# Seven products for eight in the first product of a second feed-forward layer, with streamed operands

## The chip, the core and the metric

The program runs on one core of a Trainium2 chip. The metric is the device time of one execution, in microseconds (us), as a median over runs. The core has five engines that run side by side and wait for each other by semaphores: TensorE (PE, with PEld for the loading of its stationary operand), VectorE (DVE), ScalarE (ACT), GpSimd (POOL) and SyncE (SP), which issues the transfers here. The matrix products go to eight banks of PSUM (128 partitions x 512 float32 each); all else lies in SBUF or in DRAM.

## The reference

An attention is followed by two feed-forward layers on 2304 tokens; the change is in the second layer alone. Its first product sums over 512 inputs, its second over 2048.

```python
'moe2': n_tokens, d_model, d_ff = (2304, 512, 2048)

def _moe2_ref(x, w_in, w_out):
    h = x @ w_in
    sp = np.where(h > 20.0, h, np.log1p(np.exp(np.minimum(h, 20.0))))
    g = h * np.tanh(sp)
    return (g @ w_out).astype(np.float32)
```

The first layer has the same sizes with `g = h / (1 + exp(-1.702 h))`. The weights are float64 in DRAM; the kernel sees them as pairs of 32-bit words.

## The kernel before

**Precision.** Each operand of a product is split into a high part (rounded to the matmul's float32r form) and a low part (the rest). A product of two operands is three matmuls: high by high, high by low, low by high. A "unit" is what one f (one of 16 blocks of 128 of the 2048 hidden columns) does for one block of tokens.

**Layers 1 and 2.** Both walk over five blocks of tokens, 512, 512, 512, 512 and 256, and in each over the 16 f. The first product of f (`mm_h`, L538) is 12 matmuls: four chunks of the 512 inputs (K) by three, into one of four PSUM banks h0 to h3. The second product is 12 matmuls too (L583 in layer 1, L957 in layer 2) into four accumulators tb0 to tb3, which add up over the 16 f. In layer 1 a unit h1(f) is followed, two units later, by o1(f); between them ScalarE and VectorE make `g` and split it (L564 to L570). In layer 2 the f go in pairs (G = 2): VectorE copies h out of its bank (L901) and cuts it at 20 (L904), ScalarE takes exp, log and, one pair later, tanh (L919, with a load of a function table at two of the three), VectorE multiplies and splits (L929 to L936), and the second product of a pair comes DEPTH = 3 pairs behind its first. At a block's end the accumulators are copied (L969) and stored (L972).

**Weights.** The 16 pairs of tiles wh(f), wl(f), called W0 to W15 below, lie in SBUF: each holds 512 columns for the first product and 512 for the second. The weights of layer 1 are converted from the float64 words (`conv_w`): SP loads them into a raw buffer `sr`; ScalarE writes a value and a remainder (L397, L399); VectorE clips and shifts (L403, L406), GpSimd adds (L409), VectorE sets the sign (L411); all on 128x1024, in a value buffer `sv`. ScalarE rounds it to wh (L417) and VectorE subtracts to wl (L419). There are three `sr` and three `sv` (NSR, NSV); x's blocks come through `sv` too (`load_x`, L516 to L525). From unit D0 = 16 of layer 1 on, one f of layer 2's weights every D1 = 2 units is converted as well and stored in DRAM (w2_d); at the end of layer 1 they are loaded again and split into W0 to W15, which then hold all of layer 2's weights for the rest.

**Order.** A planner, `Order`, sets the order of instructions on every engine: each operation is added with an engine, an estimated duration, what it reads and writes, and a rank; `run()` simulates the engines and, when one is free, takes the ready operation of the least rank. The order of SP's transfers is set in the same way. The hardware then runs each engine's list strictly in order.

Of the kernel before, what the change touches and what calls it, by code (L numbers as in the profile page):

```python
# [29 lines left out]
NSR = 3  # L30
# [4 lines left out]
DEPTH = 3  # L35
NG2 = 6
# [4 lines left out]
NOUT = 2  # L41
NHS = 5
# [7 lines left out]
D1 = 2  # L50
# [166 lines left out]
def attention_then_two_ffn_kernel(  # L217
# [59 lines left out]

    class LateRing:
# [18 lines left out]
    w2_d = dram.tile([KF, 128, 2 * DM], F32, name="w2_d")  # L297
# [17 lines left out]
    nqsc = const.tile([128, 1], F32, name="nqsc")  # L315

# [30 lines left out]
    vpool = ctx.enter_context(tc.tile_pool(name="sv", bufs=1, side="right"))  # L347
    stage_ctx = ExitStack()
    spool = stage_ctx.enter_context(tc.tile_pool(name="s", bufs=1, side="right"))
    srs = Ring(spool, "sr", NSR, [128, 4 * DM], F32)  # L350
    rbs = Ring(spool, "rb", 1, [128, T], F32)
    svs = Ring(vpool, "sv", NSV, [128, 2 * DM], F32)
    W = []
# [14 lines left out]
    def conv_w(layer, f, rank, deps=()):  # L368

        w_in, w_out = (w_in1, w_out1) if layer == 1 else (w_in2, w_out2)
        raw, kraw = srs.next()
        val, kval = svs.next()  # L380
# [3 lines left out]
        def word(i, dtype=U32):  # L384
# [3 lines left out]
        dma(lambda: nc.sync.dma_start(  # L388
            out=words[:, 0:n].rearrange("p (c n) -> p c n", c=KD),
            in_=w_in.bitcast(U32)[:, f * 256:(f + 1) * 256].rearrange("(c p) f -> p c f", p=128)),  # L390
            524288, w=[kraw], rank=rank, deps=deps)
        dma(lambda: nc.sync.dma_start(
            out=words[:, n:2 * n], in_=w_out.bitcast(U32)[f * 128:(f + 1) * 128, :]),
            524288, w=[kraw + (2,)], rank=rank, deps=deps)
        keys = [kraw, kraw + (2,)]
        add("ACT", t_act(n, psum=False) + 0.11,
# [31 lines left out]
    def stage_w2(f, rank, deps):  # L428
        first = len(sch.ops)
        val, kval = conv_w(2, f, rank, deps)  # L430
        staged.extend(range(first, len(sch.ops)))
        dma(lambda: nc.sync.dma_start(out=w2_d[f], in_=val), 524288, [kval], [("w2", f)], rank)

    def load_w2(f, rank):
        val, kval = svs.next()
        dma(lambda: nc.sync.dma_start(out=val, in_=w2_d[f]), 524288, [("w2", f)], [kval], rank)
        split_w(f, val, kval, rank)
# [4 lines left out]
        "o": LateRing("o", NOUT, [128, 512], F32),  # L442
# [33 lines left out]
    x_n = [0]  # L476

    def spread(r, kr, hp, t0, n, rank, deps):

        rb, krb = rbs.next()  # L480
        keys = []
        for b in range(B):
# [14 lines left out]
        add("DVE", t_dve(n), lambda: nc.vector.tensor_tensor(r, r, rb[:, 0:n], ALU.mult),  # L497
            keys, [krb, kr], rank, port=True)

    def load_x(layer, j, rank):  # L500
# [9 lines left out]
        for i in range(2):  # L510
            rt, kr = svs.next()
# [335 lines left out]
    def load_w1_from(fs):  # L847
# [8 lines left out]
        (ctx, "x", ("x",), "left"),  # L856
        (l1_ctx, "l1", ("x2",), "left"),
# [7 lines left out]
    for n in range(n1 + 2):  # L865
        if n < n1:
# [5 lines left out]
            if 0 <= f < KF and not r:  # L872
# [3 lines left out]
    l1 = outs + [i for i, *_ in x_stores]  # L876


    G = 2
    NG = KF // G  # L880
    opened2 = add("SP", 0.0, open_late([l1_ctx, stage_ctx], [
        (ctx, "l2", ("m", "hs", "o"), "left"), (ctx, "g2", ("g2h", "g2l"), "right"),
    ]), deps=l1 + staged, rank=-10.0)
    cnt = [n1]
    g2 = {}
    pending = []
    BIG2 = 2e4

    def h2(j, k, rank):
        n = blocks[2][j][1]  # L890
        unit = []
        for i in range(G):
            bank, kb = hbanks[cnt[0] % 4]
            cnt[0] += 1
            f = k * G + i
            add("PE", t_mm(n, 3 * KD), lambda bank=bank, f=f: mm_h(bank, 2, j, f),
                xt[2, j][1] + [("wh", f), ("wl", f)], [kb], rank, outs[-1:], steps=3 * KD)
            m, km = late["m"].next()
            bank = lambda bank=bank: hb[bank][:, 0:n]
            hs, khs = late["hs"].next()  # L900
            add("DVE", t_dve(n), lambda hs=hs, bank=bank: nc.vector.tensor_copy(hs()[:, 0:n], bank()),  # L901
                [kb], [khs], rank - 4.0, [opened2])
            add("DVE", t_dve(n, True),
                lambda m=m, hs=hs: nc.vector.tensor_scalar_min(m()[:, 0:n], hs()[:, 0:n], 20.0),  # L904
                [khs], [km], rank, port=True)
            unit.append((hs, khs, m, km, n))
        soft(rank, [(m, km, n) for _, _, m, km, n in unit])
        pending.append((j, k, unit))

    def soft(rank, new):  # L910

        old = [(m, km, n) for _, _, u in pending for _, _, m, km, n in u]

        for load, fn, bias, ms in (
            (1.3, AF.Tanh, 0.0, old), (0.0, AF.Exp, 0.0, new), (1.3, AF.Ln, 1.0, new)
        ):
            def go(fn=fn, bias=bias, ms=ms):
                for m, _, n in ms:
                    nc.scalar.activation(m()[:, 0:n], m()[:, 0:n], fn, bias=bias)  # L919

            if ms:
                add("ACT", load + sum(t_act(n, psum=False) for _, _, n in ms), go,
                    [], [km for _, km, _ in ms] + ["table"], rank)
        for j, k, unit in pending:
            for i, (hs, khs, m, km, n) in enumerate(unit):
                gh, kgh = late["g2h"].next()
                gl, kgl = late["g2l"].next()
                add("DVE", t_dve(n),
                    lambda m=m, hs=hs, n=n: nc.vector.tensor_tensor(  # L929
                        m()[:, 0:n], m()[:, 0:n], hs()[:, 0:n], ALU.mult),  # L930
                    [khs], [km], rank, port=True)
                add("DVE", t_dve(n, True),
                    lambda m=m, gh=gh, n=n: nc.vector.tensor_copy(gh()[:, 0:n], m()[:, 0:n]),
                    [km], [kgh], rank, port=True)
                add("DVE", t_dve(n),
                    lambda m=m, gh=gh, gl=gl, n=n: nc.vector.tensor_tensor(  # L936
                        gl()[:, 0:n], m()[:, 0:n], gh()[:, 0:n], ALU.subtract),
                    [km, kgh], [kgl], rank, port=True)
                g2[j, k, i] = (gh, gl, [kgh, kgl])
        pending.clear()  # L940

    def o2(j, k, rank):
        t0, n = blocks[2][j]
        nt = n // 128
        units = [g2.pop((j, k, i)) for i in range(G)]
        order = [(i, range(nt)) for i in range(G)]
        if k == NG - 1:
            order = [(i, (t,)) for t in range(nt) for i in range(G)]
        for i, ts in order:
            gh, gl, kg = units[i]  # L950
            f = k * G + i

            def mm(f=f, ts=ts, gh=gh, gl=gl):
                oh, ol = (parts(w)[1] for w in W[f])
                for t in ts:
                    for i, (x, w) in enumerate(((gh(), oh), (gh(), ol), (gl(), oh))):
                        nc.tensor.matmul(  # L957
                            accs[t][0], x[:, t * 128:(t + 1) * 128], w,
                            start=(f == 0 and i == 0), stop=(f == KF - 1 and i == 2),
# [4 lines left out]
            outs.append(add("PE", 3 * len(ts) * t_mm(512), mm, kg + [("wh", f), ("wl", f)],  # L964
                [accs[t][1] for t in ts], rank, steps=3 * len(ts)))
        if k == NG - 1:
            for t in range(nt):
                o, ko = late["o"].next()
                add("DVE", t_dve(512), lambda o=o, t=t: nc.vector.tensor_copy(o(), accs[t][0]),  # L969
                    [accs[t][1]], [ko], rank)  # L970
                r0 = t0 + t * 128
# [3 lines left out]
    load_x(2, 0, BIG2 - 100)  # L975
    for f in range(KF):
        load_w2(f, BIG2 - 50 + f)
    tot = NB * NG
    for n in range(tot + DEPTH):
        if n < tot:  # L980
            j, k = divmod(n, NG)
            h2(j, k, BIG2 + n)
            if k == 1 and j + 1 < NB:
                load_x(2, j + 1, BIG2 + n)
        elif pending:
            soft(BIG2 + n, [])
        if n >= DEPTH:
            o2(*divmod(n - DEPTH, NG), BIG2 + n)
# [56 lines left out]
```

## Time and profile before

| | |
|---|---|
| median of 3 runs | 1073.39 us (1072.85 to 1073.39) |
| profiled execution | 1072.84 us, span of its instructions 1071.0 us |
| TensorE busy | 1058.1 us, 99% of the span |
| VectorE, ScalarE, GpSimd busy | 685.8, 643.7, 162.5 us |
| granted TensorE clock | at its upper level through the span |

The rows below come from that one execution. Matmuls are pipelined, so their busy times overlap; the pace of a unit is read from the chain or from the distance between starts. Idle time of an engine that nothing waits for costs nothing.

### The profile page before, as it was taken

How to read it: one execution, taken by the hardware profiler on the slowest of the kernel's cores; microseconds unless marked ns; L12 is line 12 of the kernel's file. 1: busy time of each engine (PE TensorE's matmuls, PEld its weight loads, DVE VectorE, ACT ScalarE, POOL GpSimd, SP SyncE). 2: the span in 40 equal slices, each digit the busy share in tenths (PEclk: the TensorE clock that was granted, in tenths of full speed). 3: DMA queues.
4: the chain of work that ended last, by engine and by line, in shares of the span. 5: the costliest groups of instructions: out<-in, count | busy, mean ns of one | idle time of the engine just before them, and what ended most of it. 6: DMA issues, size and time to landing. Idle time of an engine off the chain costs nothing.

```text
span 1071.0 us, 16239 instructions
## 1 busy us (share of the span) xinstructions
PE 1058.1 (99%) x6060; PEld 843.4 (79%) x6060; DVE 685.8 (64%) x1380; ACT 643.7 (60%) x1025; POOL 162.5 (15%) x182
## 2 busy tenths in 40 slices
PE   9999999999999999999999999999999999999998
PEld 6666666666788888888888899888888888888887
DVE  7888999999887455446542246665555464645544
ACT  5777888798765344344432245786556656564665
POOL 1112343453443022202200000000000000000000
PEclk9999999999999999999999999999999999999999
DMA  3214343342452465465440035400000010010010
GB/s 111 97 62 150 106 172 99 123 148 83 142 167 89 147 193 180 138 215 167 154 143 1 1 119 179 156 1 30 12 28 1 10 40 1 1 40 1 1 40 21
DMA packets 51871, 95.50 MB, mean 89 GB/s; under 512 B 7888, under 2 KB 28496, under 8 KB 51792
## 3 DMA queue, kind: packets, MB, share of 16 engines
q1 hardware_dynamic: 51792, 94.47, 26.5%
q8 instruction: 47, 0.77, 0.3%
q14 instruction: 32, 0.26, 0.1%
HBM read 71.83 MB, written 22.62 MB: 88 GB/s over the span
## 4 chain that ended last, share of the span: by engine, by line
PE 90%; DVE 5%; ACT 2%; issue 2%; POOL 0%; DMA 0%; DVEq 0%; ACTq 0%; POOLq 0%
PE h L538 36%; PE tb L583 18%; PE tb L957 18%; PE sc L646 6%; PE tb L758 5%; PE tb L720 5%; DVE p L679 2%; DVE ss L669 2%; PE tb L783 1%; ACT pm L735 1%; ACT p L676 1%; PE tb L715 1%; PE tb L549 0%; DVE sv L403 0%; ACT pmt L735 0%
## 5 line engine op out<-in xcount | busy, mean ns | idle before, releaser
L919 ACT ACTIVATE ms<-ms 128x512 f32<-128x512 f32 (+1 forms) x240 | 131.3, 583 | 129.5 <-DVE ms L904 128.5
L538 PE MATMUL h<-xa,wh 128*128 128x512 f32 (+1 forms) x640 | 181.7, 368 | 0.0
L538 PE MATMUL h<-x,wh 128*128 128x512 f32 (+1 forms) x640 | 181.0, 368 | 0.0
L564 ACT ACTIVATE t<-h 128x512 f32<-128x512 f32 (+1 forms) x80 | 44.4, 555 | 148.0 <-PE h L538 147.6
L538 PEld LDWEIGHTS h<-x,wh 128*128 128x128 f32 x640 | 116.5, 188 | 20.6
L538 PEld LDWEIGHTS h<-xa,wh 128*128 128x128 f32 x640 | 116.0, 189 | 20.6 <-issue 0.4
L679 DVE SCALAR_TENSOR_TENSOR p<-ss,nm,p 128x577 f32<-128x577 f32 x144 | 122.7, 876 | 12.7 <-ACT p L676 10.0
L567 DVE SCALAR_TENSOR_TENSOR h<-t,h 128x512 f32<-128x512 f32 (+1 forms) x80 | 51.2, 640 | 115.3 <-ACT t L564 115.3
L929 DVE TENSOR_TENSOR ms<-ms,hs 128x512 f32<-128x512 f32 (+1 forms) x80 | 50.1, 635 | 116.4 <-ACT ms L919 116.2
L583 PE MATMUL tb<-gl,wh 128*128 128x512 f32 (+1 forms) x320 | 117.8, 368 | 0.0
L538 PE MATMUL h<-xa,wl 128*128 128x512 f32 (+1 forms) x320 | 117.7, 368 | 0.0
L583 PE MATMUL tb<-gh,wh 128*128 128x512 f32 (+1 forms) x320 | 117.7, 368 | 0.0
L538 PE MATMUL h<-x,wl 128*128 128x512 f32 (+1 forms) x320 | 117.7, 368 | 0.0
L583 PE MATMUL tb<-gh,wl 128*128 128x512 f32 (+1 forms) x320 | 117.7, 368 | 0.0
L676 ACT ACTIVATE p<-ss,nm 128x576 f32<-128x576 f32 x144 | 109.3, 791 | 12.6 <-DVE ss L669 12.5
L669 DVE TENSOR_SCALAR_CACHE_REDUCE ss<-sc,nqsc 128x576 f32<-128x576 f32 x144 | 111.5, 811 | 5.8 <-PE sc L646 5.2
L409 POOL TENSOR_TENSOR sv<-sv,sr 128x1024 uint32<-128x1024 uint32 x32 | 83.8, 2618 | 203.3 <-DVE sv L406 148.2
L957 PE MATMUL tb<-wh,g2h 128*128 128x512 f32 x288 | 112.1, 389 | 0.0
L957 PE MATMUL tb<-wl,g2h 128*128 128x512 f32 x288 | 112.1, 389 | 0.0
L957 PE MATMUL tb<-wh,g2l 128*128 128x512 f32 x288 | 112.0, 389 | 0.0
L673 POOL TENSOR_SCALAR nm<-nm,tau_p 128x1 f32<-128x1 f32 x144 | 78.1, 544 | 173.2 <-DVE ss L669 170.4
L919 ACT ACT_TABLE_LOAD x80 | 102.6, 1283 | 1.4
(64 smaller groups left out, 1665.5 us busy)
## 6 DMA issues: line engine op xcount, KB each, us to landing
sr<-in_w_in SPq DMA_DIRECT2D x32, 512.0 KB
sr<-in_w_out SPq DMA_DIRECT2D x32, 512.0 KB
kq<-in_kq SPq DMA_DIRECT2D x16, 576.0 KB
sv<-x_d SPq DMA_DIRECT2D x16, 512.0 KB
w_d<-sv SPq DMA_DIRECT2D x16, 512.0 KB
sv<-w_d SPq DMA_DIRECT2D x16, 512.0 KB
vr<-in_v SPq DMA_DIRECT2D x16, 384.0 KB
x_d<-xo SPq DMA_DIRECT2D x16, 288.0 KB
```

Source lines behind the costliest of these rows:

```text
L409: lambda: nc.gpsimd.tensor_tensor(bits, bits, word(0), ALU.add), keys, [kval], rank, port=True)
L538: nc.tensor.matmul(hb[dst][:, 0:n], a[:, c, :], x[:, lo, c, 0:n], start=(i == 0), stop=(i == 3 * KD - 1))
L583: nc.tensor.matmul(accs[e][0][:, 0:n], a[:, es], b()[:, 0:n], start=(f == 0 and i == 0), stop=(f == KF - 1 and i == 2), skip_group_check=True,
L646: nc.tensor.matmul(sc[i][at:at + m, g, c0:c0 + n], kq2[rows, q0:q0 + m], kq2[rows, k0:k0 + n], start=True, stop=True)
L669: lambda: nc.vector.tensor_scalar(n3, s3, nqsc, None, ALU.mult, ALU.min, accum_out=nm[:, 0:1]),
L673: lambda: nc.gpsimd.tensor_scalar(nm[:, 1:2], nm[:, 0:1], tau_p, 0.0, ALU.add, ALU.add),
L676: lambda: nc.scalar.activation(p[:, at:at + S], ns[:, 4:4 + S], AF.Exp, bias=nm[:, 0:1], scale=-1.0),
L679: lambda: nc.vector.scalar_tensor_tensor(p[:, whole], ns[:, 3 + i:4 + S + i], nm[:, 1:2], p[:, whole], ALU.is_le, ALU.mult, accum_out=sums ...
L720: nc.tensor.transpose(tb[bank][:, c0:c0 + 128], pair[:, a:a + 128], ident)
L758: nc.tensor.matmul(av[64 * i:64 * i + 64], vr[:, vc:vc + 64], p[:, a:a + 256], start=(c == 0), stop=(c == 4))
L919: nc.scalar.activation(m()[:, 0:n], m()[:, 0:n], fn, bias=bias)
L957: nc.tensor.matmul(accs[t][0], x[:, t * 128:(t + 1) * 128], w, start=(f == 0 and i == 0), stop=(f == KF - 1 and i == 2), skip_group_check= ...
```

## The change

Layer 2 takes three blocks of 768 tokens in place of five. One step of it is a pair of f (k = 0 to 7) of one block. The 512 inputs, the 256 hidden columns of the pair and the 768 tokens are each cut in half, so a step's first product is a 2 x 2 by 2 x 2 product of blocks, and is made by seven block products in place of eight (a Strassen scheme in Winograd's form). The weights' operands a11, a12, ... and their sums and differences are formed while layer 1 runs (`stage_w2`), split into high and low pieces of 256 columns and stored in DRAM (wi_d); the second product's weights go to wo_d in the same form. x's seven operands are formed at each block's start (`load_xs`) in the tiles W2 to W8. For every step SP loads the seven weight operands, 3584 columns in four transfers (`load_in`), and the second product's weights in two (`load_out`), into three and two groups of the old weight tiles.

A product is two K chunks by three matmuls of 384 columns. It adds to one of two banks, h0 and h1; VectorE takes the values out with copies or with additions to kept intermediates (u1, u2, u4). The second product of a step has six accumulators (128 tokens each): tb0 to tb3, and the two other h banks. It follows its first product by DEPTH = 2 steps; the products and the groups of six matmuls of the second product alternate by their ranks. The functions work on 768 columns.

`sr` shrinks from three buffers to two, and of the three `sv` two serve conversions from the 8th f on (`sv_w`) and one x (`sv_x`). Staging takes a pair of f each D1 = 4 units.

```diff
-NSR = 3
+NSR = 2
-DEPTH = 3
-NG2 = 6
+DEPTH = 2
+HALF = 384
-D1 = 2
+D1 = 4
...
+    sv_w, sv_x = Part(svs, (0, 1)), Part(svs, (2,))
...
+        ), rank, deps, svs if f < early else sv_w)
...
+        def piece(src, kval, dst, key):
+            t, kt = wps.next()
+            p = t.bitcast(F32R).rearrange("p (h n) -> p h n", h=2)
+            hi, lo = p[:, 0], p[:, 1]
...
+            add("ACT", t_act(256, psum=False), lambda: nc.scalar.copy(hi, src), [kval], [kt], rank)
+            add("DVE", t_dve(256), lambda: nc.vector.tensor_tensor(lo, src, hi, ALU.subtract),
+                [kval, kt], [kt + (1,)], rank, port=True)
...
+        one(0, a11)
+        one(1, a12)
+        one(5, a22)
+        mix(a22, a21, a22, ALU.add)
+        one(4, a22)
+        mix(a21, a11, a21, ALU.subtract)
+        one(3, a21)
+        mix(a11, a22, a11, ALU.subtract)
+        one(2, a11)
+        mix(a12, a12, a11, ALU.subtract)
+        one(6, a12)
...
+        put(0, b11)
+        put(1, b21)
+        put(6, b22)
+        sub(b11, b12, b11)
+        put(4, b11)
+        sub(b12, b22, b12)
+        put(3, b12)
+        sub(b22, b22, b11)
+        put(2, b22)
+        sub(b21, b21, b22)
+        put(5, b21)
...
+        def mm(p, dst, start):
+            t = wt(INS[n % 3][p // 2])[0]()[:, p % 2 * 512:p % 2 * 512 + 512]
+            w = t.rearrange("p (h c f) -> p h c f", h=2, c=2)
+            xh, xl, _ = xs[s, p]
+            i = 0
+            for c in range(2):
+                cs = slice(c * HALF, (c + 1) * HALF)
+                for h, x in ((0, xh), (0, xl), (1, xh)):
+                    nc.tensor.matmul(dst(), w[:, h, c], x()[:, cs], start=(start and i == 0), stop=(p in (5, 6) and i == 5),
+                                     skip_group_check=True)
...
+        product(0, a, ka, True)
+        u1 = keep()
+        product(1, b, kb, True)
+        h(0, 0, b, kb, *u1)
+        product(2, a, ka, False)
+        u2 = keep()
+        product(3, b, kb, True)
+        product(4, a, ka, False)
+        u4 = keep()
+        h(1, 1, b, kb, *u4)
+        product(6, a, ka, False)
+        h(0, 1, a, ka)
+        product(5, b, kb, False)
+        h(1, 0, b, kb, *u2)
...
+            if n + 2 < tot:
+                load_in(n + 2, BIG2 + n)
+            h2(n, BIG2 + n - (LS if n >= tot - LN else 0))
+            if n % KP == KP - 1 and n + 1 < tot:
+                load_xs(n // KP + 1, BIG2 + n - 2)
```

Rows of the order show how the planner places it: an engine's instructions one behind the other, line, operation, output<-inputs, shape. First VectorE in block 0 of layer 1, where the conversions of W12 and W13 meet; before:

```order
L403 TENSOR_SCALAR sv0_99<-sv0_99 128x1024
L411 SCALAR_TENSOR_TENSOR sv2_101<-sr0_95,sv2_101 128x1024
L567 SCALAR_TENSOR_TENSOR h0_2694<-t0_121,h0_2694 128x512
L406 TENSOR_SCALAR sv0_99<-sv0_99 128x1024
L419 TENSOR_TENSOR wl12_2904<-sv2_101,wh12_2903 128x1024
L570 TENSOR_TENSOR gl2_128<-h0_2694,gh2_125 128x512
```

The clip (L403) and the shift (L406) of W13, in sv0, stand ahead of the sign (L411) and the split (L419) of W12, in sv2. In the changed kernel these lines are L410, L413, L418 and L426, and x's split is L573:

```order
L410 TENSOR_SCALAR sv1_107<-sv1_107 128x1024
L426 TENSOR_TENSOR wl12_2892<-sv0_106,wh12_2891 128x1024
L413 TENSOR_SCALAR sv1_107<-sv1_107 128x1024
L573 TENSOR_TENSOR x0_2909<-sv2_108,x0_2909 128x1024
L615 SCALAR_TENSOR_TENSOR h3_2702<-t1_126,h3_2702 128x512
L618 TENSOR_TENSOR gl2_132<-h3_2702,gh2_129 128x512
L418 SCALAR_TENSOR_TENSOR sv1_107<-sr1_101,sv1_107 128x1024
L426 TENSOR_TENSOR wl13_2894<-sv1_107,wh13_2893 128x1024
```

The clip and the shift of W13, in sv1, now stand on either side of the split of W12, in sv0, and W12's sign stands ahead of both; x's split and the rows of a GELU come before W13's sign. Next TensorE in the middle of layer 2, where a first product meets a second product. Before, the last of a unit's first product and the start of a second product:

```order
L538 MATMUL h3_2697<-x0_2914,wh7_116 128x512 x2
L538 MATMUL h3_2697<-x0_2914,wl7_117 128x512
L957 MATMUL tb0_76<-wh0_102,g2h0_5560 128x512
L957 MATMUL tb0_76<-wl0_103,g2h0_5560 128x512
L957 MATMUL tb0_76<-wh0_102,g2l0_5566 128x512
L957 MATMUL tb1_77<-wh0_102,g2h0_5560 128x512
```

In the changed kernel L1036 is the first product and L1132 the second; wh3 and wl3 hold an operand of x, wh0 and wl0 the streamed weights, wh14 a split `g`:

```order
L1132 MATMUL tb1_78<-wh14_2895,wh15_2897 128x512 x2
L1132 MATMUL tb1_78<-wh14_2895,wl15_2898 128x512
L1036 MATMUL h1_2700<-wh3_115,wh0_109 128x384
L1036 MATMUL h1_2700<-wl3_116,wh0_109 128x384
L1036 MATMUL h1_2700<-wh3_115,wh0_109 128x384 x2
L1036 MATMUL h1_2700<-wl3_116,wh0_109 128x384
L1036 MATMUL h1_2700<-wh3_115,wh0_109 128x384
L1036 MATMUL h0_2699<-wh4_117,wl0_110 128x384
L1036 MATMUL h0_2699<-wl4_118,wl0_110 128x384
```

The products go in turns to h1 and h0 between groups of the second product. Last SP in the middle of layer 2. Before, it loads x from x2_d and stores results:

```order
L516 DMA sv2_101<-x2_d_73 128x2x512
L516 DMA sv0_99<-x2_d_73 128x2x256
L972 DMA out_0<-o0_5555 128x512
L972 DMA out_0<-o1_5556 128x512
```

Now the queue carries the loads of the steps between them:

```order
L1002 DMA wh0_109<-wi_d_75 128x1024
L1002 DMA wl0_110<-wi_d_75 128x1024
L1010 DMA wh14_2895<-wo_d_76 128x1024
L1002 DMA wl1_112<-wi_d_75 128x512
L1002 DMA wh1_111<-wi_d_75 128x1024
L1010 DMA wl14_2896<-wo_d_76 128x1024
```

Beside these: in TensorE's order of layer 1, o1(11), o1(12) and o1(13) now stand between h1(13) and h1(14) of the first block, and a unit of the next block before h1(15). At the start of layer 2, 18 products stand between layer 1's last unit and the first group of a second product, step 0's last product being the 7th of them; at the end five groups and a full second product stand between the last product and the last step's second product.

## Rows read from the trace of the kernel before

**Rows 1.** The page's first lines: busy time, share of the span and instructions.

```profile
span 1071.0 us, 16239 instructions
...
PE 1058.1 (99%) x6060; PEld 843.4 (79%) x6060; DVE 685.8 (64%) x1380; ACT 643.7 (60%) x1025; POOL 162.5 (15%) x182
```

**Rows 2.** Chain that ended last, in order of time: start us, us, what.

```profile
290.49 2.72 PE h L538 x12
...
674.10 21.79 PE h L538 x96
...
1005.97 2.87 PE h L538 x24
...
1056.34 10.92 PE tb L957 x48
```

**Rows 3.** Stretch: us; busy of PE, PEld, DVE, ACT, POOL; PEclk, DMA, GB/s.

```profile
675.00:680.00 5.00, 5.00 (x24) 4.14 (x23) 1.90 (x3) 2.00 (x3) 0.00 (x0) 1.00 0.96 295
```

**Rows 4.** Groups by line and form: xcount | busy us, mean ns | idle before.

```profile
L919 ACT ACTIVATE ms<-ms 128x512 f32<-128x512 f32 x192 | 113.5, 626 | 114.3 <-DVE ms L904 113.4
L919 ACT ACT_TABLE_LOAD x80 | 102.6, 1283 | 1.4
L901 DVE COPY hs<-h 128x512 f32<-128x512 f32 x64 | 44.1, 690 | 32.5 <-PE h L538 32.5
...
L904 DVE TENSOR_SCALAR ms<-hs 128x512 f32<-128x512 f32 x64 | 26.6, 420 | 0.0
L919 ACT ACTIVATE ms<-ms 128x256 f32<-128x256 f32 x48 | 17.9, 411 | 15.2 <-DVE ms L904 15.0
L525 DVE TENSOR_TENSOR x<-sv,x 128x1024 fp32r<-128x1024 f32 x8 | 9.7, 1222 | 2.7 <-ACT x L523 2.7
...
L901 DVE COPY hs<-h 128x256 f32<-128x256 f32 x16 | 6.8, 424 | 17.5 <-PE h L538 17.3
...
L904 DVE TENSOR_SCALAR ms<-hs 128x256 f32<-128x256 f32 x16 | 4.6, 290 | 0.3
```

**Rows 5.** Timeline of SyncE's queue, then stretches of half a microsecond.

```profile
742.24 1.50 SPq L516 DMA_DIRECT2D sv<-x_d  x2
...
829.49 0.38 SPq L516 DMA_DIRECT2D sv<-x_d  x1
...
746.00:746.50 0.50, 0.50 (x3) 0.39 (x3) 0.31 (x1) 0.50 (x2) 0.00 (x0) 1.00 0.24 84
...
831.50:832.00 0.50, 0.50 (x4) 0.42 (x3) 0.00 (x0) 0.50 (x1) 0.00 (x0) 1.00 0.38 131
```

**Rows 6.** Stretches in layer 1.

```profile
300.00:325.00 25.00, 25.00 (x112) 20.68 (x111) 22.33 (x27) 17.89 (x23) 10.30 (x4) 1.00 0.46 157
290.00:620.00 330.00, 330.00 (x1458) 273.25 (x1457) 171.76 (x225) 139.55 (x196) 62.80 (x24) 1.00 0.40 132
```

**Rows 7.** Timeline of one conversion, and a late clip: start us, us, what.

```profile
299.98 1.22 DVE L411 SCALAR_TENSOR_TENSOR sv<-sr,sv 128x1024 uint32<-128x1024 uint32 x1
301.11 0.69 DVE L403 TENSOR_SCALAR sv<-sv 128x1024 f32<-128x1024 f32 x1
301.23 1.06 ACT L417 CAST wh<-sv 128x1024 fp32r<-128x1024 f32 x1 [0.40 <-DVE sv L411]
...
303.42 3.00 POOL L409 TENSOR_TENSOR sv<-sv,sr 128x1024 uint32<-128x1024 uint32 x1 [3.90 <-ACT sr L399]
...
324.97 2.33 DVE L403 TENSOR_SCALAR sv<-sv 128x1024 f32<-128x1024 f32 x1
```

**Rows 8.** Timeline of VectorE's splits (L419) of W7, W12, W13 and W14.

```profile
291.36 1.81 DVE L419 TENSOR_TENSOR wl<-sv,wh 128x1024 fp32r<-128x1024 f32 x1
...
323.22 1.23 DVE L419 TENSOR_TENSOR wl<-sv,wh 128x1024 fp32r<-128x1024 f32 x1
...
330.16 1.23 DVE L419 TENSOR_TENSOR wl<-sv,wh 128x1024 fp32r<-128x1024 f32 x1
...
336.07 1.22 DVE L419 TENSOR_TENSOR wl<-sv,wh 128x1024 fp32r<-128x1024 f32 x1
```

More of the change, by code (lines that the diff above doesn't have):

```diff
@@ L40 @@
 NSS = 6
-NOUT = 2
 NHS = 5
@@ L276, in next, with __init__ @@
             return self.tiles[i], (self.name, i)
+    class Part:
+        def __init__(self, ring, which):
+            self.ring, self.which, self.n = ring, which, 0
+        def next(self):
+            i = self.which[self.n % len(self.which)]
+            self.n += 1
+            return self.ring.tiles[i], (self.ring.name, i)
     class LateRing:
@@ L366, in attention_then_two_ffn_kernel, with conv_w @@
     cmax = float(np.uint32((1151 << 20) - 2).view(np.float32)) / 8
[L368 to L378 removed]
+    def conv_w(loads, rank, deps=(), vals=svs):
         raw, kraw = srs.next()
[L380 removed]
+        val, kval = vals.next()
         words = raw.bitcast(U32)
@@ new lines, in mix, with one @@
+        def mix(out, x, y, op):
+            add("DVE", t_dve(256), lambda: nc.vector.tensor_tensor(out, x, y, op), [], [ku], rank, port=True)
+        def one(p, x):
+            piece(x, ku, wi_d[k][:, 512 * p:512 * p + 512], ("wi", k, p))
+        one(0, a11)
[8 more added lines that the diff above has]
+        mix(a12, a12, a11, ALU.subtract)
@@ L481, in spread @@
         keys = []
+        first = len(sch.ops)
         for b in range(B):
@@ L498, in spread @@
             keys, [krb, kr], rank, port=True)
+        spreads.extend(range(first, len(sch.ops)))
     def load_x(layer, j, rank):
@@ L510, in load_x @@
         for i in range(2):
-            rt, kr = svs.next()
+            rt, kr = (sv_x if layer == 1 and j else svs).next()
             krs = [kr + (0,), kr + (1,)]
@@ new lines, in load_in, with load_out @@
+    def load_in(n, rank):
+        k = n % KP
+        for q, i in enumerate(INS[n % 3]):
+            t, kt = wt(i)
+            m = min(1024, 3584 - 1024 * q)
+            dma(lambda t=t, q=q, m=m: nc.sync.dma_start(
+                out=t()[:, 0:m].bitcast(F32), in_=wi_d[k][:, 1024 * q:1024 * q + m]),
+                340 * m, [("wi", k, p) for p in range(2 * q, min(2 * q + 2, 7))], [kt], rank)
+    def load_out(n, rank):
+        k = n % KP
+        for q, i in enumerate(OUTS[n % 2]):
+            t, kt = wt(i)
+            dma(lambda t=t, q=q: nc.sync.dma_start(out=t().bitcast(F32), in_=wo_d[k][:, 1024 * q:1024 * q + 1024]),
+                340 * 1024, [("wo", k, 2 * q), ("wo", k, 2 * q + 1)], [kt], rank)
@@ L885, in attention_then_two_ffn_kernel, with h2, product, h @@
+    PO = (0, 1, 2, 3, 4, 6, 5)
+    sring, sn = (("t", 0), ("t", 1), ("keep", 0)), [0]
     g2 = {}
+    gn, on = [0], [0]
     pending = []
[L887 to L908, printed above, removed]
+    def h2(n, rank):
+        s, k = divmod(n, KP)
+        hs = [late["hs"].next() for _ in range(2)]
+        ms = [late["m"].next() for _ in range(2)]
+        at = 2 * n if n < DEPTH else 0
+        a, b = (lambda: hb[at][:, 0:HALF]), (lambda: hb[at + 1][:, 0:HALF])
+        ka, kb = hbanks[at][1], hbanks[at + 1][1]
+        def mm(p, dst, start):
[8 more added lines that the diff above has]
+                                     skip_group_check=True)
+                    i += 1
+                    yield
+        def product(p, dst, kd, start):
+            add("PE", t_mm(HALF, 6) + 0.03, lambda: mm(p, dst, start),
+                xs[s, p][2] + [wt(INS[n % 3][p // 2])[1]], [kd], rank + PO[p] / 8, steps=6)
+        def h(i, j, x, kx, y=None, ky=None):
+            (ht, kh), (mt, km) = hs[i], ms[i]
+            cs = slice(j * HALF, (j + 1) * HALF)
+            if y is None:
+                fn = lambda: nc.vector.tensor_copy(ht()[:, cs], x())
+            else:
+                fn = lambda: nc.vector.tensor_tensor(ht()[:, cs], x(), y(), ALU.add)
+            add("DVE", t_dve(HALF), fn, [kx] + ([ky] if ky else []), [kh + (j,)], rank - 4.0, [opened_hs])
+            add("DVE", t_dve(HALF, True),
+                lambda: nc.vector.tensor_scalar_min(mt()[:, cs], ht()[:, cs], 20.0),
+                [kh + (j,)], [km + (j,)], rank, [opened_m], port=True)
+        def keep():
+            name, i = sring[sn[0] % 3]
+            sn[0] += 1
+            c = lambda: (kept if name == "keep" else late[name].tiles[i])[:, 0:HALF]
+            add("DVE", t_dve(HALF), lambda: nc.vector.tensor_copy(c(), a()), [ka], [(name, i)], rank - 4.0)
+            return c, (name, i)
+        product(0, a, ka, True)
[12 more added lines that the diff above has]
+        h(1, 0, b, kb, *u2)
+        unit = list(zip(hs, ms))
+        soft(rank, [m for _, m in unit])
+        pending.append((n, unit))
@@ L910, in soft @@
     def soft(rank, new):
-        old = [(m, km, n) for _, _, u in pending for _, _, m, km, n in u]
+        old = [m for _, u in pending for _, m in u]
         for load, fn, bias, ms in (
@@ L917, in go @@
             def go(fn=fn, bias=bias, ms=ms):
-                for m, _, n in ms:
-                    nc.scalar.activation(m()[:, 0:n], m()[:, 0:n], fn, bias=bias)
+                for m, _ in ms:
+                    nc.scalar.activation(m(), m(), fn, bias=bias)
             if ms:
[L922 to L939, printed above, removed]
@@ L940, in soft @@
-        pending.clear()
[L942 to L949, printed above, removed]
+                add("ACT", load + sum(t_act(2 * HALF, psum=False) for _ in ms), go,
+                    [], [km + (j,) for _, km in ms for j in range(2)] + ["table"], rank)
@@ L950, in o2, with mm @@
+        pending.clear()
+    acc2 = accs + [((lambda i=i: hb[i]), hbanks[i][1]) for i in (2, 3)]
+    def o2(n, rank):
+        s, k = divmod(n, KP)
+        units = [g2.pop((n, i)) for i in range(2)]
+        if k == KP - 1:
+            order = [(i, (t,)) for t in range(6) for i in range(2)]
+        else:
+            order = [(i, (t, t + 1)) for i in range(2) for t in range(0, 6, 2)]
+        for q, (i, ts) in enumerate(order):
             gh, gl, kg = units[i]
-            f = k * G + i
-            def mm(f=f, ts=ts, gh=gh, gl=gl):
-                oh, ol = (parts(w)[1] for w in W[f])
+            w, kw = wt(OUTS[n % 2][i])
+            def mm(i=i, ts=ts, gh=gh, gl=gl, w=w):
+                oh, ol = w()[:, 0:DM], w()[:, DM:2 * DM]
```

187 lines of the change are left out of this document (134 added, 53 removed).

## The prediction

> **What bounds the kernel now.** The page's busy shares come first: TensorE is busy 99% of the span, VectorE 64% and ScalarE 60% [rows 1]. A share that high can still hide waits, so the chain that ended last comes next: from 290.49 us on it is TensorE alone, one unit of matmuls behind the other without a gap [rows 2]. The reader should see there that a unit of 12 matmuls of 512 columns always takes 2.72 us (226.7 ns each), that 24 of 256 columns take 2.87 us (119.6 ns each), and that layer 2 runs from 674.10 to 1067.26 us, 393.2 us. The counts give the same: first product 768 x 226.7 ns + 192 x 119.6 ns = 197.1 us, second product 864 x 226.7 ns = 195.9 us, together 393.0. So in layer 2 a matmul saved is time saved, as long as nothing makes TensorE wait. Behind the last matmul stand a copy and a store, which the change leaves alone.
>
> **Fewer columns.** The first product becomes 3 blocks x 8 pairs x 7 products x 6 matmuls = 1008 matmuls of 384 columns. The trace has none in this layer's form; the nearest rows are 119.6 ns (256 columns) and 226.7 ns (512). Taken at 2.4 GHz (the granted clock is 1.00, [rows 3]) these are 106.7 + 12.9 and 213.3 + 13.4: a column costs a cycle, a matmul 13 ns more. I take 160 + 13.2 = 173.2 ns, so 174.5 us, **22.5 us less** than 197.1. The second product keeps its 864 matmuls.
>
> **Layer 2 beside TensorE.** A step (seven products, 36 matmuls of the second product) is 42 x 173.2 + 36 x 226.7 ns = 15.43 us. VectorE has seven reads of 384 columns from PSUM (0.56 us, halfway between 0.424 and 0.690), four minima (0.36), four operations on 768 columns (0.96, between 0.69 and 1.22) and two casts (0.56): 10.3 us. ScalarE has six functions on 768 columns (0.84) and two table loads (1.28): 7.6 us [rows 4]. Both fit. What could wait is the bank: two PSUM banks, h0 and h1, take turns, and a product that adds to h0 needs the copy of h0 that VectorE makes behind the product before. That turn costs 0.56 us and some 0.1 us at each end, at worst 1.6 us where a 0.96 us operation is in front. The order shows that between two products into the same bank stands at least one product into the other (6 x 173.2 ns = 1.04 us), and nearly always a group of the second product too (6 x 226.7 ns = 1.36 us). So it is hidden; uncovered it would be 24 x (1.6 - 1.04) = 13 us with one bad turn in each step. I take 0.5 us. The chain from a step's last product to its last second-layer operand is 0.56 + 0.36 + 0.84 + 1.28 + 1.68 + 1.28 + 1.68 + 2 x (0.96 + 0.56 + 0.96) = 12.6 us; with DEPTH 2 a whole step, 15.43 us, covers it, and at the end five groups and a full second product, 5 x 1.36 + 8.16 = 15.0 us. At the start of layer 2, 18 products (18.7 us) stand between the last unit of layer 1 and the first second product, which follows step 0's last product by 11.4 us and may wait up to 1.2 us: I take 0.5 us.
>
> **The streamed operands.** Each step loads 3584 + 2048 columns of 512 bytes, 2.88 MB in six transfers, and with x and the results 3.3 MB per 15.43 us, 212 GB/s. At the hand-over of the layers the queue moved 295 GB/s for 5 us while 24 matmuls ran in those 5 us, the usual pace [rows 3]. SP waits in order, but each load is for a step later than the next one, so it has some 15 us; two loads of 512 KB, issued from 742.24 us, were through by 746.5 [rows 5]. Cost: nothing, hidden under a step of matmuls; uncovered, below as a rival.
>
> **Layer 1, the staging.** Now ScalarE and VectorE also split 88 pieces of 256 columns and VectorE makes 32 differences: 88 x 0.41 = 36 us on ScalarE, 120 x 0.42 = 50 us on VectorE, at the lengths of the 256-column rows [rows 4]. Between 290 and 620 us they are busy 139.6 and 171.8 of 330 us [rows 6]. What hides this is the distance from h1(n) to o1(n), four units (10.9 us) for a chain of four operations on 512 columns, at 0.63 to 0.69 us some 2.7 us. I take nothing; if these queues fell behind it would cost as below.
>
> **Layer 1, its first weights.** This is where I expect a loss. With two raw and two value buffers (of three), the next f's clipping stands behind the split of the f before in VectorE's order; before, the clipping and the combination of the next f came ahead of it. So a conversion is nearly serial: 0.69 + 0.69 (two clips) + 3.0 (GpSimd) + 1.22 + 1.06 + 1.22 = 7.9 us [rows 7, 8], and with a pair of the GELU's rows between, about 8.9 us; with x's rows too, 9.9. Before, splits finished 5.9 to 6.9 us apart, and W13 was split at 331.4 us and needed at 344.9 [rows 2, 8]. Now W8 cannot begin before W7's split has freed its value buffer (293 us, [rows 8]), so it is ready near 302, and Wf at 302 + 8.9 (f - 8). The units h1(f) start at 290.49 + 5.44 (f - 3). W12: 337.6 against 339.4, in time. W13: 346.5 against 344.9, 1.6 us late. Then o1(11), o1(12), o1(13) stand ahead of h1(14), so W14 (355.4) is in time, and W15 (364.3 against 361.2 + 1.6) is 1.5 us late: **3 us**. At 7.9 us per f nothing is late; at 9.9 W12, W13 and W15 are late by 2.2, 4.4 and 3.5 us, together 10.
>
> **Sum.** -22.5 + 0.5 + 0.5 + 3 = -18.5 us. The profiled execution took 1072.84 us (span 1071.0), 0.5 us under the median of the runs shown: 1054.3 us, or 1054.8 from the median. I say **1054.5**. Its own range is 1049.5 (nothing waits) to 1061 (layer 1 at its bound).
>
> **Rivals.** (1) *The stream binds, slower.* Were the transfers of a step to land one after the other, a step would cost six times a transfer; one of 256 KB alone was through in 2.5 us, two of 512 KB together in 4.2 [rows 5]. It decides at 393.2 / 24 = 16.4 us per step, 2.7 us a transfer; at 3.0 us a step takes 18 us and layer 2 432: 1112 us. For it: one queue, in order. Against: the overlap in those rows, and 295 GB/s. Chance 0.05. The Trainium skill (DMA: Bandwidth & Descriptors, Anatomy of one DMA) gives a DMA about 2.0 us plus its bytes at 436 GB/s; by that, an estimate, 3.2 us for 512 KB, 18.6 us a step and some 1126 us if none overlapped, but the two loads above agree only with overlap. (2) *Two banks are too few, slower.* If each of the 168 products waited on its bank, 0.134 us a product would eat the gain; at 0.3 us it is 50 us and 1100. For it: products used four banks before. Against: the 1.04 to 2.40 us of cover above. Chance 0.04. (3) *Layer 1 falls behind.* The staging or the first weights cost 10 to 20 us: 1061 to 1071. For it: at 300 to 325 us VectorE is busy 22.3 of 25 us [rows 6], and a clip that met GpSimd took 2.33 us instead of 0.69 [rows 7]. Against: the slack between units. Chance 0.13. (4) *A matmul's cost is mostly fixed, no change.* If 384 columns took 195.5 ns, 1008 of them would be the old 197.1 us: 1073. Against: the 256-column rows take 0.53 of the 512-column ones. Chance 0.04, with all that ends there. The Trainium skill (TensorE: Matmul & The Clock Gate, Back-to-back issue gap) gives a sustained spacing of 81 ns for 128 columns and 131 ns for 512; on a line through these, an estimate, the products would go from 119.4 to 115.2 us and save 4 us. The trace's 226.7 and 119.6 ns disagree with it.
>
> **Chances and range.** The forecast (1049.5 to 1061) 0.74. A difference under 0.2% (2.1 us) is about what a measurement of this kernel cannot tell from none. Faster: 0.74 and rival 3's 0.13, 0.87; the same: 0.04; slower: rivals 1 and 2, 0.09. The range 1049.5 to 1067 leaves out the upper part of rival 3 (0.05), rivals 1, 2 and 4 (0.13) and a little below.
>
> **What would show it.** The 384-column units of six near 1.04 us; layer 2 about 371 us from its first product to its last matmul; TensorE's waits on a weight split (the lines of wh and wl in layer 1) some 3 us in all, between 335 and 370 us; next to nothing on VectorE's copies from h0 or on transfers from wi_d and wo_d. The prediction is wrong if these last two appear in every step, if a 384-column matmul costs near 195 ns, or if layer 1 grows by more than 10 us.

## The result and the profile after

The changed kernel takes 1055.66 us (median of 4 runs, 1055.37 to 1056.23) against 1073.36 us: a ratio of 0.9837, 95% interval 0.982 to 0.9854. The forecast was 1054.5. The profiled execution took 1055.78 us, 17.06 less than that of before. First the page's head, which answers to [rows 1]:

```profile
span 1054.0 us, 16947 instructions
...
PE 1041.0 (99%) x6108; PEld 851.7 (81%) x6108; DVE 769.8 (73%) x1515; ACT 608.6 (58%) x980; POOL 158.4 (15%) x182
```

TensorE is still the bound; VectorE has 84 us more to do and in layer 2 TensorE waits for it once. The chain in order of time (start us, us, what) shows where layer 1 ends and what layer 2 is made of:

```profile
291.20 2.72 PE h L586 x12
...
345.60 2.72 PE h L586 x12
...
356.48 8.26 PE h L586 x36
...
670.37 2.88 PE tb L631 x24
...
739.25 2.08 PE h L1036 x12
741.34 1.39 PE tb L1132 x6
742.73 1.04 PE h L1036 x6
...
754.89 2.08 PE h L1036 x12
...
777.48 2.76 PE tb L1132 x12
780.25 2.10 PE h L1036 x12
...
1042.18 5.44 PE tb L1132 x24
```

Compare it with [rows 2] in four stretches. The unit that began at 290.49 us begins at 291.20: +0.7. From there to layer 2: 383.6 us before; after, the first product starts at 673.25 with one unit of layer 1 (1.43 us) still to come behind it, so 383.5: -0.1. Layer 2 to the last matmul's end: 393.2 before, 375.7 after: -17.5. Behind it -0.1. Together -17.0.

So layer 1 lost nothing, and layer 2 gained 17.5 us where I had 21.5. Its 1008 products' matmuls run at 1.04 / 6 = 173.3 ns, as forecast. What was not forecast stands in the groups of the second product: six matmuls take 1.39 us, not 6 x 226.7 ns = 1.36; twelve take 2.76, not 2.72, and the twelve products' matmuls behind them 2.10, not 2.08; but the 24 at the end, with no product between, take 5.44, exactly 226.7 each. A step is 7 x 1.04 + 6 x 1.39 = 15.62 us (from 739.25 to 754.89: 15.64) against my 15.43.

TensorE's waits in layer 2 and for the first weights, from the lists of who waited for whom (us in total, times, longest), and TensorE's and the transfers' load in the middle of layer 2 (columns as [rows 3]):

```profile
PE h L1036 <- DVE hs L1051: 0.3, 1, 0.3
...
PEld h L586 <- DVE wl L426: 0.2, 1, 0.2
```

```profile
700.00:1000.00 300.00, 300.00 (x1496) 269.82 (x1496) 208.76 (x362) 152.00 (x166) 0.00 (x0) 1.00 0.64 197
```

TensorE is never idle in these 300 us, at 197 GB/s. The four microseconds are not a wait; they lie in the pace of the matmuls.

### The profile page after: what moved, and what is told of

It is laid out like the page before. It is cut to its first block, busy times and chain, and to the rows that moved or that the text cites. A ratio compares the mean times of both kernels' runs of the same rounds, so it can differ in the third digit from the quotient of the medians.

```text
span 1054.0 us, 16947 instructions
## 1 busy us (share of the span) xinstructions
PE 1041.0 (99%) x6108; PEld 851.7 (81%) x6108; DVE 769.8 (73%) x1515; ACT 608.6 (58%) x980; POOL 158.4 (15%) x182
## 4 chain that ended last, share of the span: by engine, by line
PE 94%; ACT 3%; DVE 2%; issue 1%; POOL 0%; DVEq 0%; ACTq 0%; POOLq 0%
PE h L586 19%; PE tb L631 19%; PE h L1036 16%; PE tb L1132 13%; PE sc L694 7%; PE tb L806 6%; PE h L1132 6%; PE tb L768 6%; PE tb L831 1%; ACT pm L783 1%; DVE ss L717 1%; ACT p L724 1%; DVE p L727 1%; PE tb L763 1%; PE tb L597 0%
## 5 line engine op out<-in xcount | busy, mean ns | idle before, releaser
L1091 ACT ACTIVATE ms<-ms 128x768 f32<-128x768 f32 x144 | 116.3, 841 | 154.4 <-DVE ms L1054 153.8
L1036 PE MATMUL h<-wh,wh 128*128 128x384 f32 x384 | 112.0, 334 | 0.0
L721 POOL TENSOR_SCALAR nm<-nm,tau_p 128x1 f32<-128x1 f32 x144 | 78.6, 546 | 173.3 <-DVE ss L717 170.9
L586 PE MATMUL h<-xa,wh 128*128 128x512 f32 (+1 forms) x384 | 102.9, 355 | 0.0
L783 ACT COPY pm<-tb 128x512 f32<-128x512 f32 x144 | 79.3, 592 | 34.2 <-PE tb L768 33.7
L694 PE MATMUL sc<-kq 64*128 64x288 f32 (+3 forms) x672 | 93.5, 414 | 1.3 <-DVE ss L717 1.3
L768 PEld LDWEIGHTS tb<-ident,p 128*128 128x128 f32 x576 | 62.0, 141 | 29.2 <-issue 13.6
L1036 PE MATMUL h<-wh,wl 128*128 128x384 f32 x288 | 84.1, 335 | 0.3 <-DVE hs L1051 0.3
L768 PE MATMUL tb<-ident,p 128*128 128x128 f32 x576 | 81.9, 280 | 1.8 <-ACT pm L783 1.2
L586 PE MATMUL h<-x,wh 128*128 128x512 f32 x256 | 78.8, 389 | 0.0
L1036 PEld LDWEIGHTS h<-wh,wh 128*128 128x128 f32 x384 | 71.0, 188 | 2.9
```

What stands on the lines that cost most here:

```text
L586: nc.tensor.matmul(hb[dst][:, 0:n], a[:, c, :], x[:, lo, c, 0:n], start=(i == 0), stop=(i == 3 * KD - 1))
L694: nc.tensor.matmul(sc[i][at:at + m, g, c0:c0 + n], kq2[rows, q0:q0 + m], kq2[rows, k0:k0 + n], start=True, stop=True)
L768: nc.tensor.transpose(tb[bank][:, c0:c0 + 128], pair[:, a:a + 128], ident)
L783: add("ACT", t_act(cols), lambda src=src, dst=dst: nc.scalar.copy(dst, src), [("tb", bank)], [kpn + (half,)], rank)
L1036: nc.tensor.matmul(dst(), w[:, h, c], x()[:, cs], start=(start and i == 0), stop=(p in (5, 6) and i == 5), skip_group_check=True)
L1091: nc.scalar.activation(m(), m(), fn, bias=bias)
```

## The experiments

**1. Same size for both products.** Theory A: a run of matmuls pays for the change of size. B: for the change of tiles and banks. C: the matmuls are slowed by transfers or VectorE. The edit lets each matmul of a product read 128 more columns, which nobody uses (the lines that widen the operand tiles and the output to match are left out here):

```diff
-                cs = slice(c * HALF, (c + 1) * HALF)
+                cs = slice(c * HALF, c * HALF + 512)
...
```

> The first product's matmuls read 512 columns in place of 384 (128 of them are not used), so that first and second product have one size. In the changed kernel a run of 6 second-product matmuls takes 1.389 us, 0.029 more than 6 x 226.7 ns, and a run of products 0.004 more than its matmuls. Theory A, the price belongs to the change of size between neighbouring matmuls: every run goes back to 226.7 ns a matmul, and the time is 1055.7 + 1008 x 0.0533 - 3.7 = 1105.7 us. Theory B, the price comes from the change of operand tiles and banks, whatever the size: the extra 0.03 us per run of second-product matmuls stays, and the time is near 1109.5 us. Theory C, the transfers or VectorE slow the second product's matmuls: the extra stays too.

Measured: 1104.31 us. The chain in layer 2 (L1037 the products, L1133 the second product):

```profile
767.03 2.72 PE h L1037 x12
769.75 1.36 PE tb L1133 x6
```

Every run is back at 226.7 ns a matmul, though tiles and banks change as before and VectorE and the stream go on. B and C fall; A stands. The time is 1.4 us under A's sum, for two reasons that the starts of the matmuls show: the wait at the start of layer 2 (0.7 us in the changed kernel) is gone here, and the price of the size was 4.4 us in the changed kernel (below), not 3.7.

**2. No stream.**

```diff
-            if n + 2 < tot:
+            if n == 0:
                 load_in(n + 2, BIG2 + n)
...
-            if n - DEPTH + 2 < tot:
-                load_out(n - DEPTH + 2, BIG2 + n)
```

> Leaves out the loads of the weights' operands for all steps but the first three (first product) and two (second product); the later steps compute with what lies there. TensorE's order stays. Theory A (size change): nothing moves, runs of 6 stay at 1.389 us, 1055.7 us within 0.5. Theory C (the stream slows TensorE): runs of 6 fall to 1.36 us and the time to about 1051.9 us. If loads were waited for anywhere, their waits would go as well.

Measured: 1055.98 us. The same 300 us and a group:

```profile
700.00:1000.00 300.00, 300.00 (x1497) 269.82 (x1495) 208.80 (x363) 152.01 (x166) 0.00 (x0) 1.00 0.05 16
```

```profile
741.54 1.39 PE tb L1132 x6
```

At 16 GB/s in place of 197 the groups still take 1.39 us. The stream costs nothing, as forecast, and is not the cause of the 4 us.

**3. Fewer changes of size.** One rank for a step's second-product groups:

```diff
-                rank + (q + 0.5) / len(order), steps=3 * len(ts))
+                rank + 0.55 + q / 400, steps=3 * len(ts))
```

> Second-product groups get one rank in the middle of the step, so that most steps have one run of 36 second-product matmuls and one of 42 product matmuls: 68 runs in layer 2 in place of 224 (each kind counted). Theory A: 78 pairs of switches less at 0.033 us, 2.6 us, 1053.1 us, if the banks' turns stay covered by the one product between two uses of a bank (1.04 us against 0.77 for the turn). Theories B and C (no price per change of size): no gain from the runs, 1055.7 or more. Rival: bank turns come uncovered behind longer VectorE operations, 0.3 us in each of 20 steps, 6 us: 1059.

Measured: 1055.41 us (1055.25 to 1055.51). The chain in a common step, and where a step is the first of a block:

```profile
718.67 7.30 PE h L1036 x42
725.98 2.76 PE tb L1132 x12
...
734.18 7.30 PE h L1036 x42
...
796.34 2.12 PE h L1036 x12
...
800.04 0.87 DVE ms L1102
800.91 0.48 DVE t L1061
...
801.43 1.31 PE h L1036 x6
```

The common step is 15.51 us, 0.13 less, from two runs that pay 0.026 us (42 x 173.3 ns is 7.28, and from the start of this run to the next it is 7.31) and 0.040 us. But at 800 and at 926 us a product waits for a bank:

```profile
PE h L1036 <- DVE t L1061: 1.8, 2, 0.9
```

By the starts of its matmuls each place costs 1.07 us, and 0.1 more at the matmul behind: 2.4 us in two places, and the gain is gone. The copy that frees the bank (L1061) stands behind 0.95 us of a multiplication (L1102). The gain was there; a new wait took it.

**4. A bank's turn laid open.**

```diff
-                rank + (q + 0.5) / len(order), steps=3 * len(ts))
+                rank + 0.9 + q / 400, prods[-1:], steps=3 * len(ts))
...
```

(`prods` holds the products; the lines that fill it are left out.)

> The second product of a step is held back until the step's last product, so that all seven products stand in a row and the fifth and the sixth, both in bank h0, are neighbours: the bank's turn lies open once a step. Priced as in the prediction (0.56 us for the copy and about 0.1 us at each end) it costs 24 x 0.77 = 18.5 us, less 91 pairs of switches x 0.033 = 3.0 us by theory A: 1071 us. If a 0.96 us operation of VectorE stands in front each time, 1.6 us a turn: 1091 us. If the turn is hidden all the same, 1053 us.

Measured: 1084.59 us, between the two prices. First TensorE's wait list, then the chain at one open turn, and the shortest turn in the timeline:

```profile
PE h L1037 <- DVE kept L1062: 19.5, 22, 1.2
```

```profile
744.56 0.96 DVE xa L1109
745.52 0.48 DVE kept L1062
...
746.04 2.38 PE h L1037 x12
```

```profile
796.20 0.34 PE L1037 MATMUL h<-wh,wh 128*128 128x384 f32 x1
797.18 0.44 PE L1037 MATMUL h<-wh,wl 128*128 128x384 f32 x1 [0.65 <-DVE kept L1062]
```

The shortest turn is 0.98 us from start to start, 0.81 beyond the matmul's own 0.17: my 0.77 was close to the price of the shortest turn. The common one has an operation of 0.96 us in front and takes 1.2 us from start to start. With some smaller waits it is (1084.59 - 1055.66 + 3.0) / 24 = 1.33 us a step. So two banks are enough in the changed kernel because something stands between two uses of a bank: a group of the second product, or at least a product into the other bank (1.04 us), which alone covered the turn in the common steps of run 3.

**5. The open turn covered.** The sixth product of a step is made to stand behind all its second-product groups (the second product is planned ahead of the products, and `seconds` holds its groups):

```diff
-                xs[s, p][2] + [wt(INS[n % 3][p // 2])[1]], [kd], rank + PO[p] / 8, steps=6)
+                xs[s, p][2] + [wt(INS[n % 3][p // 2])[1]], [kd], rank + PO[p] / 8, seconds[-1:] if p == 6 else [], steps=6)
...
```

> As the run with one rank for the second product's groups, and the sixth product of a step now stands behind all of them, in every step: there the two places (one at each change of block) where the fifth and sixth product were neighbours in bank h0 cost 1.2 us each. Theory A (change of size, 0.033 us a pair of switches in the changed kernel, 0.065 for long runs): 66 runs in place of 224, and no open turn: 1055.4 - 2.4 = 1053.0 us. Rival, the gain is lost to another wait once these two go: 1055.4.

Measured: 1058.76 us, a miss in both directions. The two places stayed: it is the third product there, which waits for the copy behind the first, so my reading of which neighbours met was wrong. And the last step's products now end late; its second product waits for VectorE, 2.0 and 0.8 us (the chain is then VectorE's):

```profile
1041.32 1.83 DVE ms L1103 x2
...
1045.01 5.32 PE tb L1133 x22
```

That is the chain that the prediction counted as 12.6 us under 15.0 us of cover at the end: it binds as soon as the last step's products move back.

**6. Layer 1 without the planner's new order.** For the 3 us of late weights that did not come:

```diff
-        outs.append(add("PE", t_mm(n, 3 * KD) + 0.05, mm, kg + [("wh", f), ("wl", f)], keys, rank, steps=3 * KD))
+        outs.append(add("PE", t_mm(n, 3 * KD) + 0.05, mm, kg + [("wh", f), ("wl", f)], keys, rank, steps[-1:], steps=3 * KD))
```

> Layer 1's second-product units are tied behind the first-product unit two later, so TensorE keeps the order h1(14), o1(12), h1(15), o1(13) and cannot move o1(12), o1(13) ahead. W14 is whole at 354.0 us and W15 at 362.1 in the changed kernel's trace. Theory A, the first weights are late and the planner's order hides it: h1(14) would start at 351.0 us and need the low part of W14 at 351.5, 2.6 us late, and W15 another 2.5: about 5 us longer, 1060.8 us. Rival, the weights are not close to the path: 1055.7.

Measured: 1062.51 us, 6.9 more than the changed kernel. The chain shows W14 and W15 late, and the stretches behind the first wait show more:

```profile
353.17 1.24 DVE wl L426
...
354.45 4.12 PE h L586 x10
...
362.22 1.24 DVE wl L426
...
363.50 2.57 PE h L586 x10
```

```profile
351.00:355.30 4.30, 2.00 (x7) 1.03 (x6) 3.75 (x5) 3.15 (x3) 0.00 (x0) 0.98 0.10 29
355.40:358.10 2.70, 2.70 (x8) 2.13 (x7) 1.66 (x2) 0.00 (x0) 2.24 (x1) 0.50 0.13 48
```

The waits are near the 5 us expected: by the starts of the matmuls, W14 and W15 cost two waits each, one for the high and one for the low part, 4.4 us in all. Behind the first pair, for which TensorE stood idle 2.3 of 4.3 us, the granted clock is 0.50, that is 1.2 GHz, for seven matmuls, 0.2 us each: 1.4 us more. Behind the second pair, where TensorE stood idle 1.4 of 3.5 us (361.0 to 364.5), it stayed at 1.00.

**7. The conversions made longer.**

```diff
-        ), rank, deps, svs if f < early else sv_w)
+        ), rank, deps, svs if f < early else sv_w, 1 if f < early else 2)
...
```

(the last argument is the number of clips; the loop that repeats the clip is left out)

> The clip of the conversions from the 8th f on stands twice on VectorE (the second changes nothing in the values), 0.72 us more in each. The spacing of the weights goes from 8.85 to about 9.6 us. Theory A (the conversion chain sets when a weight is ready, and the low part is needed 0.45 us behind the unit's start): with the order of this kernel W13 is 1.0 us late and W15 3.4 us, in all 4.5 to 5.5 us longer, 1060.2 to 1061.2. Rival (the waits between the chain's links absorb the clip): 1055.7.

Measured: 1059.95 us, 4.3 more: the size fits theory A, the place doesn't. TensorE hardly waited for a weight (0.2 us, W13's low part). It waited for the GELU of a unit, whose last subtraction stands on VectorE behind the longer conversion and x's rows, and the clock then fell as in the run before:

```profile
PE tb L632 <- DVE gl L619: 2.0, 1, 2.0
```

By the starts of the matmuls this wait is 2.1 us, and eight matmuls behind it (granted clock 0.66 from 356.3 to 361.0) come 0.2 us late each, 1.6 us. So it shows that this stretch has no room left on VectorE, and not that the weights set the end.

**8. The price of the change of size, in the kernel before.** Blocks of 384 tokens in layer 2, nothing else:

```diff
-    blocks = {1: [512, 512, 512, 512, 256], 2: [512, 512, 512, 512, 256]}
+    blocks = {1: [512, 512, 512, 512, 256], 2: [384] * 6}
...
```

> The kernel before with layer 2 in six blocks of 384 tokens, all else as it was: no seven-for-eight scheme, no stream. First product 1152 x 173.3 = 199.7 us in place of 197.1, second product the same 864 matmuls of 512. Theory A (a price for the change of size, 0.033 to 0.065 us a pair): 48 pairs, 1.6 to 3.1 us, 1077.3 to 1078.8 us. Without such a price: 1075.7 us.

Measured: 1079.18 us. The chain has 24 first-product matmuls of 384 columns beside 18 of 512:

```profile
812.17 4.18 PE h L538 x24
816.35 4.12 PE tb L957 x18
```

18 x 226.7 ns is 4.08 us and 24 x 173.3 is 4.16: 0.04 and 0.026 a run, with no scheme and no stream. Theory A, a little above its upper bound: 43 such pairs are 2.9 us by the starts, and the first group of the second product comes 0.5 us late.

**9 and 10. A version that keeps the gain.** The changed kernel again, and beside it on the same chip the third run's ranks, except in the first step of a later block:

```diff
-                rank + (q + 0.5) / len(order), steps=3 * len(ts))
+                rank + ((q + 0.5) / len(order) if (n + DEPTH) % KP == 0 else 0.55 + q / 400), steps=3 * len(ts))
```

> The changed kernel itself, timed beside the next one on the same chip: 1055.7 us within 0.4 by every theory. It is there for the comparison alone.

> One rank for the second product's groups as in the first run of that kind, but the first step of each later block keeps the changed kernel's ranks, since there a bank's turn stood open (1.2 us at each of two places). Theory A (0.033 us a pair of switches, 0.065 in long runs): 72 runs in place of 224 and no open turn, 1055.4 - 2.4 + 0.1 = 1053.1 us, 2.6 less than the changed kernel. Rival: other turns come open in their place, 1055.4.

Measured: 1055.49 us (1055.19 to 1055.89) and 1054.21 us (1053.61 to 1054.43; ratio to before 0.9822, interval 0.9808 to 0.9835). The two intervals of the ratio overlap, the ranges of the runs don't: 1.3 us, half of what I expected. The timeline shows what is left of the two open turns:

```profile
799.64 0.95 DVE L1102 TENSOR_TENSOR ms<-ms,hs 128x768 f32<-128x768 f32 x1
800.51 0.55 DVE L1061 COPY t<-h 128x384 f32<-128x384 f32 x1
```

The copy is still behind the multiplication; TensorE's matmuls come 0.28 us late there and 0.11 at the next, in two places: 0.8 us of the missing 1.3. In the two profiled executions layer 2 alone is 1.6 us shorter (375.2 against 376.8, from its first matmul's start to its last one's), near the 1.8 that this leaves; but it starts 0.6 us later in run 10, and that is there from the first 13 us of the execution on, ahead of anything that the edit touches.

## Why the prediction was right, and by which errors

The time fell 1.2 us above the forecast and inside its own range. Two of its terms were wrong by 3 and 4 us, with opposite signs, and in the profiled executions 0.7 us came from ahead of layer 1's fourth unit, for which it had no term; most of that is spread between executions (see the end of this section). That the sum landed this near is luck; the 22.5 us saved, the cover and the stream are not.

**Fewer columns: right.** 173.2 ns forecast, 173.3 measured, so 174.7 us for the first product (1008 x 173.2 ns is 174.6; the prediction has 174.5). The rival that a matmul's cost is mostly fixed is out. The Trainium skill (TensorE: Matmul & The Clock Gate, Back-to-back issue gap) has 131 ns for 512 columns in a sustained stream; these traces have 226.7 ns for 512 columns and 173.3 for 384, and the measurement decides.

**The term that was missing.** The step "42 x 173.2 + 36 x 226.7 ns = 15.43 us" took each matmul at the price it has among its like. By the starts of the matmuls, a run of 512 columns behind one of 384 pays 0.018 us if it has 3 matmuls, 0.029 if it has 6 and 0.040 from 9 on, so the price builds up over its first matmuls; a run of 384 pays 0.004 behind a run of 6, and 0.026 behind one of 9 or more. In the changed kernel that is 3.5 us in the runs of 512 (93 of them have 6 matmuls) and 0.9 in the runs of 384, 4.4 together; the waits in layer 2 came to 0.7 where I had 1.0. That is layer 2's missing 4.0 within 0.1. Runs 1, 2 and 8 show that size is what matters, not stream, banks or VectorE. The trace of before had it, in the last block, where 256-column units alternate with the second product, and I did not look at a unit's neighbours; the eight runs behind 256 columns in that block pay 0.027 us each, which is the 0.2 us between the prediction's 393.0 us counted and 393.2 measured. Its chain, behind a unit of 512 and behind one of 256 columns:

```profile
1000.53 5.44 PE tb L957 x24
...
1008.84 5.47 PE tb L957 x24
```

**Layer 1's first weights: mechanism right, size wrong.** I forecast W8 near 302 us and 8.9 us per f, and 3 us of waiting. VectorE's splits of W8, W13, W14 and W15, which answer to [rows 8]:

```profile
298.88 1.23 DVE L426 TENSOR_TENSOR wl<-sv,wh 128x1024 fp32r<-128x1024 f32 x1 [1.11 <-ACT wh L424]
...
344.27 1.23 DVE L426 TENSOR_TENSOR wl<-sv,wh 128x1024 fp32r<-128x1024 f32 x1 [1.12 <-ACT wh L424]
...
352.80 1.22 DVE L426 TENSOR_TENSOR wl<-sv,wh 128x1024 fp32r<-128x1024 f32 x1 [0.52 <-ACT wh L424]
...
360.87 1.22 DVE L426 TENSOR_TENSOR wl<-sv,wh 128x1024 fp32r<-128x1024 f32 x1 [0.24 <-ACT wh L424]
```

The spacing is (360.87 - 298.88) / 7 = 8.86 us: right. But W8 was whole at 300.1, two microseconds sooner; the units began 0.7 us later than before; and the low part is first read by a unit's third matmul, 0.45 us behind its start. W13 was whole at 345.50 for a unit that began at 345.60, W15 at 362.09 for one that began near 361.9. What was left is the 0.1 us in the 8.26 us of the chain. Run 6 shows that the reordered units carry it: without them the same conversions cost 6.9 us. So the rival "layer 1 falls behind" was near, and its price is steep.

**The cover: right.** Bank turns cost 0; the start of layer 2 cost 0.7 us by the starts (0.46 at the matmul that waits, 0.10 at the one behind it, 0.11 in the first group of the second product), against 1.0 forecast for both. VectorE's and ScalarE's durations (0.56, 0.36, 0.96 and 0.84 us) came within 1%; only a split of 256 columns took 0.53 us where I had 0.42, and hurt nobody:

```profile
L1091 ACT ACTIVATE ms<-ms 128x768 f32<-128x768 f32 x144 | 116.3, 841 | 154.4 <-DVE ms L1054 153.8
...
L449 DVE TENSOR_TENSOR wp<-sv,wp 128x256 fp32r<-128x256 f32 x88 | 45.0, 526 | 6.9 <-ACT wp L448 6.7
...
L1102 DVE TENSOR_TENSOR ms<-ms,hs 128x768 f32<-128x768 f32 x48 | 44.3, 954 | 9.3 <-ACT ms L1091 9.3
...
L1054 DVE TENSOR_SCALAR ms<-hs 128x384 f32<-128x384 f32 x96 | 33.1, 357 | 1.7
L1061 DVE COPY t<-h 128x384 f32<-128x384 f32 x48 | 26.7, 556 | 30.1 <-PE h L1036 28.3
```

Rival 2's mechanism is real (run 4: 1.33 us a step) and was rightly given little chance, because the order leaves a group of the second product between two uses of a bank.

**The stream: right.** Run 2 took it away and nothing moved. By the Trainium skill's price (DMA: Bandwidth & Descriptors, Anatomy of one DMA) without overlap I had an estimate of 1126 us, 18.6 us of transfers a step. The section gives that price for transfers issued by GpSimd, and SyncE issues these; a step took 15.64 us here without a wait for one, so the trace agrees with it only if transfers overlap.

**Open.** Of the 0.7 us ahead of layer 1's fourth unit, 0.5 are there from the attention's first products on: the 21st matmul of its scores (`sc`) starts at 11.97 us before and at 12.46 after, but at 12.48 in run 8 too, which has the attention of the kernel before, and between 11.9 and 12.8 in all twelve profiles. That is spread between executions and not the change. The other 0.2 arise where the attention ends and layer 1's first units stand in another order, and no run looked at them. Why a change of size is paid for is not shown, nor why a run of 384 pays more behind a longer run of 512; only that size does it.

## What to carry to other kernels

Price a step of mixed matmuls by a stretch where they are mixed, not by sums of like with like: look in the trace for places where two sizes already alternate. Before splitting work into two alternating streams, count the alternations, and weigh longer runs against what the short ones cover: here the same groups that cost 4.4 us hide bank turns worth 32. When a forecast lands, check it term by term; this one was right to 0.1% by two errors of opposite sign.

## What had not been expected of the hardware

A change of the moving operand's columns between runs of matmuls (384 and 512) cost 0.033 us a pair in runs of 6 and 0.066 in long ones, without any idle time in the profile. And a late weight can cost more than its lateness: in run 6, behind a stall of 2.3 in 4.3 us, the granted clock stood at 0.50 for seven matmuls, 1.4 us on top; behind the next stall, 1.4 in 3.5 us, it did not fall.
